# Two halves instead of one product: normalisation by head, inverse planes in another order, the last gate in two

## The chip, the core and the metric

The kernel runs on one core of one Trainium2 chip. The metric is the device time of a run in microseconds (us). Shorter is better.

## The reference

Local attention with a few global keys, followed by a gated long convolution. Four batches, 8 heads of 64, 768 positions, model width 512. What is computed, cut to its core:

```python
keep  = (pos_k < 8) | ((0 <= rel) & (rel < 96))        # rel = pos_q - pos_k
s     = q @ k.T / 8 - slope[h] * dist                   # dist: |rel|, or 96 for a far global key
a     = softmax(where(keep, s, -1e9))
x     = (a @ v) as [batch, 768, 512]
x1, x2, x3 = split(x @ w_proj)                          # three times 512 columns
conv  = irfft(rfft(x2, axis=1) * rfft(filter, axis=0)) # length 768
out   = (x1 * conv * x3) @ w_out
```

## The kernel before

**How the work is cut.** The program is a list of some thousand pieces ("atoms"), each a handful of instructions for one engine with a cost, the pieces it needs and a due number. A planner (`Plan.order`) walks through them: for each engine it takes the piece that can start first by its own reckoning, and among those within 30 of each other the one with the smallest number in the table `DUE`. A second table, `HOME`, pins some pieces that both ScalarE (ACT) and VectorE (DVE) could do to one of them. The result is one fixed order of instructions on each engine; on the chip every engine works through its own order and waits on semaphores. PSUM is one tile, `bank`, whose eight banks the planner hands out: single banks, and pairs of banks.

**The stages of a batch b.** Names in brackets are the planner's kinds, with the lines of the profile.

- Head of the program: GpSimd (POOL) writes two index rows and issues the loads. DVE makes distances in `far` (L324 to L344: the tile `neg`, then casts into `dist`, L331 and L332, a small strip, L333, and the rows of the global keys). TensorE (PE), ACT and DVE make the sines of the Fourier matrices (`wh`, L411, is a step of it on DVE; PE multiplies it in at L415). The filter, `fl`, is loaded by POOL at L499, folded by DVE (L516 to L526), multiplied by PE (L544) and copied to `h`. After the sines ACT makes the masks from `dist` (L359, L363).
- Queries and keys are transposed by PE (L697) and copied out as `QT`, `KT` (L225 on ACT, L227 on DVE: the helper `copy` records all plain copies on these lines, those with a factor on L225 and L229).
- For each of the four pairs of heads: scores (L857; for batch 0 the distances are added by PE at L845), exponentials by ACT (L874), masks by DVE (L885, batches 1 to 3), and the values (L899, L903) into a pair of banks, one bank for each head of the pair, with the sum of each row in a 65th column. Normalising is one piece on DVE: the reciprocal of 14 sums (L914) and one product over 128x896 (L915). PE transposes the result (L946), and ACT or DVE copies it to `xT`.
- After pairs 1 and 3 DVE folds the columns of two pairs (L965 to L970, tile `xr`). PE makes x1 and x3 from `xT` (L1056, "gates"), x2 from `xr` (L991), and the forward transform (L1009); copies `x`, `ab` and `X` leave the banks on ACT or DVE. DVE multiplies the spectrum (L1028 to L1040).
- The inverse: PE writes an even and an odd half for each 128 columns (L1118), each of three planes of 128; one copy takes both halves to `eo`; DVE completes the planes and joins the halves to `y` (L1152 to L1160: a sum of planes into `es`, a correction, and four sums or differences of halves) and multiplies by the gates (L1167). In the last batch this goes column block by column block.
- PE multiplies by `w_out` (L1182); the copy `ot` and a store by SyncE (SP, L1199) end the batch.

Of the kernel before, what the change touches and what calls it, by code (L numbers as in the profile page):

```python
# [30 lines left out]
class Plan:  # L31
# [9 lines left out]
    OPEN, SWAP, STICK = 8, 95.0, 1292.892  # L41
    LONE = 24718.4
# [138 lines left out]
class Fused:  # L181
# [134 lines left out]
    def far(self, part):  # L316
# [13 lines left out]
        if part == 1:  # L330
            v.tensor_copy(dist[:, 0:3], neg[:, None, :].to_broadcast([P, 3, 216]))  # L331
            v.tensor_copy(dist[:, 3, 0:168], neg[:, 0:168])  # L332
            v.tensor_scalar(dist[:, 3, 168:216], neg[:, 72:120], self.pc, None, op0=Alu.max)  # L333
        if part == 2:
            gl = mp.tile([NG, 2, KL], F32, tag="rc2", bufs=1, name="gl")
# [102 lines left out]
    def setup(self):  # L438
# [11 lines left out]
        for p, n in enumerate((1400, 1110, 2080)):  # L450
            A["far"] = [add("DVE", n, lambda p=p: self.far(p), [A["d0"]] + A["far"], due=-9, kind=f"far.{p}")]
# [275 lines left out]
    def due_hy(self, b, off):  # L727
# [3 lines left out]
    DUE = [2.91, 1.28, 8.39, 7.23, 4.07, 5.61, 7.59, 8.65, 5.7, 13.31, 5.58, 11.66, 13.01, 11.97,  # L731
# [529 lines left out]
```

## Time and profile before

| | |
|---|---|
| median of three runs | 173.18 us (173.03 to 173.38) |
| the profiled execution: its own time | 173.39 us |
| its span, first to last instruction | 171.6 us |
| granted TensorE clock | 1.000 |
| busy in the span | PE 93%, DVE 91%, ACT 81%, POOL 45% |

The profile gives each engine's busy time, the rows of a timeline (start and duration in us, engine, line, operation, output<-input), groups of equal instructions with their mean duration, and the chain of work that ended last. On ACT and DVE the next instruction of the same engine starts a little before the recorded end of the one ahead of it, so what an instruction costs its engine is read from the distance of two starts. A matmul's recorded duration holds its way through the array, and four matmuls can be under way at once.

### The profile page before, as it was taken

What the parts mean: (1) busy time and instruction counts of PE and PEld (TensorE: products, weight loads), DVE (VectorE), ACT (ScalarE), POOL (GpSimd) and SP (SyncE); (2) the same over time, 40 slices, a digit from 0 to 9 for tenths busy, and PEclk for the clock granted to TensorE, in tenths of its full rate; (3) what the DMA queues carried; (4) which work ended last, traced back from release to release, by engine and by line L of the source; (5) the groups of instructions that cost most, each with busy time, mean ns of one, the idle gap of its engine ahead of it and who ended that gap; (6) DMA issues with size and microseconds to landing.
All of it is one profiled execution on the core that took longest, in us unless ns stands there. A gap on an engine that the chain in (4) does not pass through costs nothing.

```text
span 171.6 us, 4147 instructions
## 1 busy us (share of the span) xinstructions
PE 159.0 (93%) x1595; PEld 94.1 (55%) x1595; DVE 156.5 (91%) x365; ACT 138.8 (81%) x244; POOL 77.9 (45%) x101
## 2 busy tenths in 40 slices
PE   5398979889999999999999999999999999999990
PEld 2046437675445777644566775454657754457630
DVE  7899989899999999999999999999999999999830
ACT  4479989899886849889997778988998988868751
POOL 8992885533999958632497768210000000000000
PEclk9999999999999999999999999999999999999999
DMA  3999999999999999999999999999921100062036
GB/s 47 152 149 186 125 178 182 206 205 159 123 116 118 130 136 146 106 160 126 129 150 215 165 184 164 108 101 150 271 97 65 63 0 0 35 253 85 0 132 234
DMA packets 81731, 22.97 MB, mean 134 GB/s; under 512 B 71536, under 2 KB 78640, under 8 KB 81712
## 3 DMA queue, kind: packets, MB, share of 16 engines
q0 software_dynamic: 64208, 12.81, 119.8%
q1 hardware_dynamic: 17504, 9.90, 31.0%
q8 instruction: 12, 0.20, 0.5%
q14 instruction: 7, 0.06, 0.1%
HBM read 25.59 MB, written 6.29 MB: 186 GB/s over the span
## 4 chain that ended last, share of the span: by engine, by line
PE 70%; DVE 23%; ACT 1%; issue 1%; POOL 1%; DVEq 0%; POOLq 0%; ACTq 0%
PE bank L1056 21%; PE bank L991 12%; PE bank L1182 10%; PE bank L1118 5%; PE bank L1009 5%; DVE xn L915 4%; PE bank L857 3%; PE bank L899 3%; DVE E L885 3%; PE bank L946 3%; PE bank L903 2%; PE bank L697 2%; DVE KT L227 2%; DVE QT L227 2%; PE bank L845 2%; PE bank L544 2%
## 5 line engine op out<-in xcount | busy, mean ns | idle before, releaser
L1056 PE MATMUL bank<-xT,w 128*128 128x384 f16 x256 | 47.6, 326 | 0.1
L874 ACT ACTIVATE E<-bank 128x864 f16<-128x864 f32 x48 | 41.1, 906 | 1.3 <-PE bank L857 1.3
L617 POOL DMA_DIRECT2D vb<-in_v_dram x32 | 27.2, 851 | 21.2 <-DMA vb<-in_v_dram 12.2
L1056 PEld LDWEIGHTS <-w 128*128 128x128 f16 x256 | 24.2, 98 | 16.6 <-issue 0.9
L225 ACT ACTIVATE x<-bank 128x384 f16<-128x384 f32 x52 | 25.9, 507 | 6.2 <-PE bank L1056 4.6
L991 PE MATMUL bank<-w,xr 128*128 128x512 f16 x96 | 23.1, 380 | 0.0
L1182 PE MATMUL bank<-wo,y 128*128 128x512 f16 x96 | 23.0, 379 | 0.0
L885 DVE TENSOR_TENSOR E<-E,mask 128x864 f16<-128x864 f16 x36 | 20.9, 599 | 0.4 <-ACT E L874 0.3
L915 DVE TENSOR_TENSOR xn<-bank,rc 128x896 f16<-128x896 f32 x16 | 17.5, 1092 | 0.6
L225 ACT ACTIVATE ot<-bank 128x512 f32<-128x512 f32 x22 | 13.2, 611 | 5.4 <-PE bank L1182 4.2
L225 ACT CAST ab<-bank 128x512 f16<-128x512 f32 x24 | 14.0, 594 | 3.6 <-PE bank L991 3.5
L663 POOL DMA_DIRECT2D q<-in_q_dram x16 | 13.6, 853 | 5.0 <-DMA wo<-in_moe_w_out_dram 1.8
L899 PEld LDWEIGHTS <-E 128*128 128x128 f16 x224 | 14.0, 98 | 2.0
L857 PE MATMUL bank<-QT,KT 64*128 64x216 f16 (+2 forms) x224 | 14.5, 242 | 0.7 <-ACT E L874 0.7
L663 POOL DMA_DIRECT2D k<-in_k_dram x16 | 13.8, 864 | 2.5 <-DMA k<-in_k_dram 2.2
L899 PE MATMUL bank<-vb,E 128*128 128x65 f16 x224 | 14.8, 193 | 0.0
L225 ACT CAST X<-bank 128x512 f16<-128x512 f32 x23 | 13.0, 603 | 2.1 <-PE bank L1009 2.0
L991 PEld LDWEIGHTS <-xr 128*128 128x128 f16 x96 | 8.9, 98 | 10.3 <-issue 0.9
L1182 PEld LDWEIGHTS <-y 128*128 128x128 f16 x96 | 9.0, 98 | 9.7 <-DVE y L1167 0.6
L903 PE MATMUL bank<-vb,E 128*128 128x65 f16 x192 | 14.3, 193 | 0.0
L225 ACT CAST eo<-bank 128x768 f16<-128x768 f32 x16 | 12.6, 812 | 1.7 <-PE bank L1118 1.6
L857 PEld LDWEIGHTS <-KT 64*128 64x128 f16 x224 | 7.9, 94 | 10.1 <-issue 6.8
(135 smaller groups left out, 298.0 us busy)
## 6 DMA issues: line engine op xcount, KB each, us to landing
out_dram<-ot SPq DMA_DIRECT2D x24, 256.0 KB, 2.3
vb<-in_v_dram POOLq DMA_DIRECT2D x32, 90.0 KB, 10.3
w<-in_moe_w_proj_dram POOLq DMA_DIRECT2D x3, 512.0 KB, 12.7
q<-in_q_dram POOLq DMA_DIRECT2D x16, 96.0 KB, 8.3
k<-in_k_dram POOLq DMA_DIRECT2D x16, 90.0 KB, 7.6
k<-in_k_dram POOLq DMA_DIRECT2D x4, 192.0 KB, 4.5
q<-in_q_dram POOLq DMA_DIRECT2D x4, 192.0 KB, 5.8
fl<-in_moe_filter_fft_dram POOLq DMA_DIRECT2D x1, 768.0 KB, 9.8
```

What stands on the lines that cost most here:

```text
L225: nc.scalar.copy(dst, src) if scale is None else nc.scalar.mul(dst, src, scale)
L617: g.dma_start(x[NG:P, 0:6, h, 0:D], self.v[b, h, 0:6 * KL].rearrange("(t p) d -> p t d", p=KL))
L663: g.dma_start(tile()[NG * j:P, i, 0:6, D * hh:D * hh + D], x.rearrange("(t p) d -> p t d", t=6))
L857: nc.tensor.matmul(sp[:, hh, off:off + w], KT[64 * hh:64 * hh + 64, o:o + P], QT[64 * hh:64 * hh + 64, KL * m:KL * m + w], start=(off == 0 ...
L874: nc.scalar.activation(eo, self.t["s", n, gi][:, :, 0:432].rearrange("p h (m w) -> p h m w", m=2), Act.Exp, scale=self.scale)
L885: nc.vector.tensor_mul(eo, eo, mk)
L899: nc.tensor.matmul(oc, ef[:, c:c + P], vt[:, t, 2 * i + hh, :], start=(t == 0), stop=(t == 0), skip_group_check=True)
L903: nc.tensor.matmul(oc, ef[:, c:c + P], vt[:, t - 1, 2 * i + hh, :], start=False, stop=True, skip_group_check=True)
L915: nc.vector.tensor_mul(xn.rearrange("p t h d -> p h t d"), o[:, :, :, 0:D], rc.to_broadcast([P, 2, 7, D]))
L991: nc.tensor.matmul(pt, T["xr", b][:, 2 * c + t // 3, t % 3], self.w[:, c, DM:2 * DM], start=(c == 0), stop=(c == 3))
L1056: nc.tensor.matmul(pt[:, 0:h], self.w[:, c, o + P * j:o + P * j + P], T["xT", b][:, c, h * s:h * s + h], start=(c == 0), stop=(c == 3))
L1182: nc.tensor.matmul(T["o", b, t], T["y", b][:, c, P * t:P * t + P], self.wo[:, c, :], start=(c == 0), stop=(c == 3))
```

## The change

Five edits, and two new tables. The constants `STICK` and `LONE` of the planner and both tables, `DUE` and `HOME`, are replaced as a whole, so the order on every engine differs nearly everywhere, though each piece's needs are the same but for the edits.

1. Normalising is three pieces: the reciprocal (still one, on DVE), and one product for each head of the pair, on DVE or on ACT. On ACT a product is seven instructions of 128x64 with the reciprocal as a scale read by each partition.
2. The two casts of the distances may go to ACT (`self.copy`), and the strip is a piece of its own.
3. The inverse's matmuls write their double plane to planes 0 and 2 and the single one to plane 1, so that joining the halves is three instructions in place of four.
4. In the last batch the last column block's copy to `eo` is two pieces, and its joining and gate are two parts, "a" for the planes 0 and 2 and "b" for plane 1.
5. The six output tiles of the last batch come in the order 1, 4, 0, 3, 2, 5.

```diff
-    OPEN, SWAP, STICK = 8, 95.0, 1292.892
-    LONE = 24718.4
+    OPEN, SWAP, STICK = 8, 95.0, 1434.540
+    LONE = 34987.8
...
-            v.tensor_copy(dist[:, 0:3], neg[:, None, :].to_broadcast([P, 3, 216]))
-            v.tensor_copy(dist[:, 3, 0:168], neg[:, 0:168])
+            self.copy(dist[:, 0:3], neg[:, None, :].to_broadcast([P, 3, 216]))
+            self.copy(dist[:, 3, 0:168], neg[:, 0:168])
+        if part == 3:
             v.tensor_scalar(dist[:, 3, 168:216], neg[:, 72:120], self.pc, None, op0=Alu.max)
...
-    DUE = [2.91, 1.28, 8.39, 7.23, 4.07, 5.61, 7.59, 8.65, 5.7, 13.31, 5.58, 11.66, 13.01, 11.97,
+    DUE = [0.69, -0.13, 5.71, 13.54, 2.85, 4.08, 8.43, 6.13, 11.65, 12.87, 3.67, 6.19, 7.33,
...
-            nc.vector.reciprocal(rc, o[:, :, :, D:D + 1])
-            nc.vector.tensor_mul(xn.rearrange("p t h d -> p h t d"), o[:, :, :, 0:D],
-                                 rc.to_broadcast([P, 2, 7, D]))
+            nc.vector.reciprocal(rc, o[:, :, :, D:D + 1])
...
+                if self.cur.eng == "ACT":
+                    for t in range(7):
+                        nc.scalar.activation(xn[:, t], o[:, t, 0:D], Act.Copy, scale=rc[:, t])
+                else:
+                    nc.vector.tensor_mul(xn, o[:, :, 0:D], rc.to_broadcast([P, 7, D]))
...
-                            nc.tensor.matmul(pt[:, P * lo:P * lo + P * n], xt(s), m, start=(s > 1 and s % 2 == 0),
+                            o3 = pt[:, 0:3 * P].rearrange("p (t m) -> p t m", t=3)
+                            nc.tensor.matmul(o3[:, 0:3:2] if n == 2 else o3[:, lo], xt(s), m, start=(s > 1 and s % 2 == 0),
...
-                    v.tensor_sub(yv[:, :, 1], eo[:, :, 0, 1], eo[:, :, 1, 1])
-                    v.tensor_add(yv[:, :, 4], eo[:, :, 0, 1], eo[:, :, 1, 1])
-                    v.tensor_add(yv[:, :, 0:3:2], eo[:, :, 0, 0:3:2], eo[:, :, 1, 0:3:2])
-                    v.tensor_sub(yv[:, :, 3:6:2], eo[:, :, 0, 0:3:2], eo[:, :, 1, 0:3:2])
+                        if part == "a":
+                            v.tensor_add(yv[:, :, 0:5:4], e[:, :, 0:3:2], o[:, :, 0:3:2])
+                            v.tensor_sub(yv[:, :, 3], e[:, :, 0], o[:, :, 0])
+                            v.tensor_sub(yv[:, :, 1], e[:, :, 2], o[:, :, 2])
+                        elif part == "b":
+                            v.tensor_add(yv[:, :, 2], e[:, :, 1], o[:, :, 1])
+                            v.tensor_sub(yv[:, :, 5], e[:, :, 1], o[:, :, 1])
+                        else:
+                            v.tensor_add(yv[:, :, 0:6:2], e, o)
+                            v.tensor_sub(yv[:, :, 3:6:2], e[:, :, 0:2], o[:, :, 0:2])
+                            v.tensor_sub(yv[:, :, 1], e[:, :, 2], o[:, :, 2])
...
-        for t in range(6):
+        for k, t in enumerate((1, 4, 0, 3, 2, 5) if fine and b in self.THRICE else range(6)):
```

What the order becomes at three places. First the head of the program, on DVE, from the distances to the last step of the sines (`wh`); `idm` are scaled identities, `gl` the rows of the global keys. Before:

```order
L328 TENSOR_TENSOR neg<-neg,d_96 128x216
L349 MEMSET E_70 128x2x6x16
L350 MEMSET E_70 128x2x80
L411 TENSOR_SCALAR wh<-th 128x512
L411 TENSOR_SCALAR wh<-th 128x256
L331 CAST dist<-neg 128x648
L332 CAST dist<-neg 128x168
L333 TENSOR_SCALAR dist<-neg,pc 128x48
L411 TENSOR_SCALAR wh<-th 128x512
L336 TENSOR_SCALAR gl<-d_96 8x120
```

And now:

```order
L328 TENSOR_TENSOR neg<-neg,d_96 128x216
L412 TENSOR_SCALAR wh<-th 128x256
L350 MEMSET E_72 128x2x6x16
L351 MEMSET E_72 128x2x80
L355 TENSOR_SCALAR idm<-ident 128x128 x4
L334 TENSOR_SCALAR dist<-neg,pc 128x48
L355 TENSOR_SCALAR idm<-ident 128x128 x2
L412 TENSOR_SCALAR wh<-th 128x512 x2
L355 TENSOR_SCALAR idm<-ident 128x128 x2
L337 TENSOR_SCALAR gl<-d_96 8x120
```

The two casts have left DVE; they stand on ACT between its first and second step of the sines. Second, the same stretch on POOL, which issues the loads one after the other (`q`, `k`, `vb` are the first batch's queries, keys and values, `fl` the filter). Before:

```order
L304 IOTA row 1x384
L588 DMA k_89<-in_k_dram 128x2x384
L300 IOTA d_96 128x216
L588 DMA k_89<-in_k_dram 128x2x384 x2
L604 DMA vb_85<-in_v_dram 8x8x64
L446 MEMSET k_90 8x512
L588 DMA q_87<-in_q_dram 128x2x384 x2
L499 DMA fl<-in_moe_filter_fft_dram 128x6x512
```

And now:

```order
L589 DMA q_87<-in_q_dram 128x2x384
L304 ISA
L304 IOTA row 1x384
L300 IOTA d_96 128x216
L589 DMA k_89<-in_k_dram 128x2x384
L589 DMA q_87<-in_q_dram 128x2x384
L589 DMA k_89<-in_k_dram 128x2x384 x2
L447 MEMSET k_89 8x512
L605 DMA vb_85<-in_v_dram 8x8x64
L612 DMA vb_85<-in_v_dram 120x8x64
L500 DMA fl<-in_moe_filter_fft_dram 128x6x512
```

A load of queries now stands ahead of the first index row, and one more load of values (`120x8x64`, 120 KB on the page) stands ahead of the filter. Third, the last two normalisations of the last batch, on DVE (`E` the exponentials under their mask, `g` the gates). Before:

```order
L1082 TENSOR_TENSOR g<-x 128x768
L885 TENSOR_TENSOR E_72<-E_72,mask 128x2x2x216 x2
L914 RECIPROCAL rc<-bank 128x14
L915 TENSOR_TENSOR xn<-bank,rc 128x2x7x64
L914 RECIPROCAL rc<-bank 128x14
L915 TENSOR_TENSOR xn<-bank,rc 128x2x7x64
L1082 TENSOR_TENSOR g<-x 128x768
```

And now, first DVE, then ACT from the first of that batch's halves on it:

```order
L889 TENSOR_TENSOR E_72<-E_72,mask 128x2x2x216 x3
L918 RECIPROCAL rc<-bank 128x14
L930 TENSOR_TENSOR xn<-bank,rc 128x7x64 x2
L918 RECIPROCAL rc<-bank 128x14
L1097 TENSOR_TENSOR g<-x 128x768
L930 TENSOR_TENSOR xn<-bank,rc 128x7x64
L229 TENSOR_SCALAR x<-bank 128x384
L227 COPY xT<-bank 128x768
```

```order
L928 ACTIVATE xn<-bank,rc 128x64 x7
L225 ACTIVATE x<-bank 128x384
L878 ACTIVATE E_70<-bank 128x2x2x216 x2
L225 ACTIVATE x<-bank 128x384 x2
L225 COPY xT<-bank 128x768
L878 ACTIVATE E_70<-bank 128x2x2x216
L928 ACTIVATE xn<-bank,rc 128x64 x7
L225 ACTIVATE x<-bank 128x384 x2
L878 ACTIVATE E_72<-bank 128x2x2x216 x3
L225 ACTIVATE x<-bank 128x384
```

One head of a pair stays on DVE and the other has gone to ACT, among the exponentials; a copy `x` and a copy `xT` have come to DVE. Over the whole program 10 of the 32 halves are on ACT (70 instructions) and 22 on DVE. In turn these copies out of the banks change engine: on DVE `ot` goes from 2 to 6, `X` from 1 to 3, `ab` from 0 to 2, `xT` from 5 to 8, `x` from 4 to 5, and the copies to `h` from 6 to 3; ACT has as many fewer or more.

More of the change, by code (lines that the diff above doesn't have):

```diff
@@ L1161, in hyena @@
-                three = b in self.THRICE
-                hv = add("DVE", (1320 if three else 1660) if one else (1970 if three else 2580), halves, need + A.get(("yfree", b - 1), []) + ys[-1:],
-                         due(20 + 4.5 * jp), kind=f"H{nm}")
-                A.setdefault(("eofree", 2 * b + jp), []).append(hv)
-                def gate(js=js):
-                    nc.vector.tensor_mul(T["y", b][:, js], T["y", b][:, js], T["g", b][:, js])
-                ys.append(add("DVE", 450 if one else 870, gate,
-                              [hv] + [gates[j, s] for j in range(js.start, js.stop) for s in range(2)],
-                              due(21 + 4.5 * jp), kind=f"Y{nm}"))
+                three = b in self.THRICE
@@ L1183, in fn @@
                                          start=(c == 0), stop=(c == 3))
-                need = [x, A["wo"]] + (ys[0:cs[-1] + 1] if fine else ys)
-                x = add("PE", 216 * len(cs), fn, need, due(27 + 0.9 * t), take=None if first else "mm",
+                last = cs[-1] + (cs[-1] == 3 and t % 3 == 2 and len(ys) == 5)
+                need = [x, A["wo"]] + (ys[0:last + 1] if fine else ys)
+                x = add("PE", 216 * len(cs), fn, need, due(27 + 0.9 * k), take=None if first else "mm",
                         kind=f"O{b}.{t}")
```

127 lines of the change are left out of this document (79 added, 48 removed), and 169 rows, old and new, of the table DUE.

## The prediction

> **What bounds the kernel now.** First the page's chain of work that ended last, by engine:
>
> ```profile
> PE 70%; DVE 23%; ACT 1%; issue 1%; POOL 1%; DVEq 0%; POOLq 0%; ACTq 0%
> ```
>
> Two engines share the bound, so an average says little. The table by stretches shows where each of them sets the pace; its columns are the length, then the busy time (and instructions) of PE, its weight loads, DVE, ACT and POOL.
>
> ```profile
> 17.60:40.70 23.10, 20.72 (x358) 13.40 (x357) 21.34 (x40) 21.23 (x38) 14.02 (x18) 1.00 1.89 181
> 40.70:44.00 3.30, 3.30 (x28) 1.80 (x28) 3.27 (x10) 2.80 (x5) 1.74 (x3) 1.00 3.63 120
> 44.00:118.00 74.00, 73.89 (x698) 43.54 (x694) 72.59 (x152) 62.00 (x108) 48.34 (x58) 1.00 2.23 141
> 118.00:134.00 16.00, 15.91 (x216) 10.27 (x213) 15.44 (x31) 14.63 (x25) 0.00 (x0) 1.00 0.79 152
> 134.00:168.00 34.00, 33.36 (x203) 18.71 (x203) 28.94 (x75) 26.27 (x48) 0.00 (x0) 1.00 0.19 72
> ```
>
> From 17.6 to 134 DVE idles 1.76 + 0.03 + 1.41 + 0.56 = 3.8 us of 116, and ACT 1.87 + 0.50 + 12.0 + 1.37 = 15.7 us. A PE that is busy there is not a PE at its peak, since a matmul is recorded longer than it holds the array. After 134 the picture turns: DVE idles 5 us, and the timeline has the last 24 products with `w_out` in one piece, then one copy and one store:
>
> ```profile
> 162.02 5.34 PE L1182 MATMUL bank<-wo,y 128*128 128x512 f16 x24
> 163.33 0.56 DVE L1167 TENSOR_TENSOR y<-y,g 128x768 f16<-128x768 f16 x1
> 167.45 0.60 ACT L225 ACTIVATE ot<-bank 128x512 f32<-128x512 f32 x1 [0.32 <-PE bank L1182]
> ```
>
> 24 products in 5.34 us, of which the last one's way through the array is a part, is 0.22 us each: nothing waits there. So I read: **to 134 us DVE's list sets the pace, with ACT behind it; after that PE's own work does**, about 34 us, then 4 us of copy and store, and none of that shrinks. The sum therefore goes over DVE's list up to the last normalisation.
>
> **The change part by part.** *Normalising.* In the last batch's timeline the next start shows what each instruction holds DVE for:
>
> ```profile
> 126.38 1.09 DVE L915 TENSOR_TENSOR xn<-bank,rc 128x896 f16<-128x896 f32 x1
> 127.40 0.61 DVE L885 TENSOR_TENSOR E<-E,mask 128x864 f16<-128x864 f16 x1
> 127.92 0.55 DVE L229 TENSOR_SCALAR x<-bank 128x384 f16<-128x384 f32 x1
> 128.39 0.41 DVE L1036 TENSOR_TENSOR X<-p,p 128x512 f16<-128x512 f16 x1
> ...
> L915 DVE TENSOR_TENSOR xn<-bank,rc 128x896 f16<-128x896 f32 x16 | 17.5, 1092 | 0.6
> ```
>
> The product takes 127.40 - 126.38 = 1.02 us for 896 elements, a copy of 384 from a bank 0.47. On the line through both, 448 elements take 0.54 (0.51 if it were plain half, 0.60 with one more start-up). So 16 x 1.02 = 16.3 becomes 22 x 0.54 = 11.9: **-4.4 us** (-5.1 to -3.1). The 16 reciprocals stay.
>
> *Copies that come to DVE.* A 512-wide one, and `xT`:
>
> ```profile
> 114.92 0.68 DVE L227 CAST X<-bank 128x512 f16<-128x512 f32 x1
> 115.52 0.68 DVE L1028 TENSOR_TENSOR p<-X,h 128x1024 f16<-128x1024 f16 x1
> ...
> 40.19 0.55 DVE L227 COPY xT<-bank 128x768 f16<-128x768 f16 x1
> 40.66 1.08 DVE L227 COPY KT<-bank 128x720 f16<-128x720 f16 x2
> ```
>
> 0.60 and 0.47 us. Up to the last normalisation DVE gets 4 `ot`, 2 `X` and 2 `ab` more, 8 x 0.60 = 4.8, two `xT` 0.94 (the third comes after it), one `x` 0.47, and three copies to `h` fewer, -1.8: **+4.4 us**. What normalising frees, other work takes.
>
> *Distances.* The casts leave DVE, where the sines waited behind them:
>
> ```profile
> 6.53 0.82 DVE L331 CAST dist<-neg 128x648 f16<-128x648 f32 x1
> ...
> 8.15 0.46 DVE L333 TENSOR_SCALAR dist<-neg,pc 128x48 f16<-128x48 f32 x1
> 8.30 0.57 DVE L411 TENSOR_SCALAR wh<-th 128x512 f16<-128x512 f32 x1
> ```
>
> Both casts lie between the first two rows, 8.15 - 6.53: **-1.6 us**. ACT takes them on; from its masks,
>
> ```profile
> L359 ACT ACTIVATE mask<-dist 128x432 f16<-128x432 f16 x8 | 4.2, 555 | 0.0
> L363 ACT ACTIVATE mask<-dist 128x216 f16<-128x216 f16 x8 | 2.8, 381 | 0.0
> ```
>
> 0.8 ns an element, about 0.9 us for both, while ACT is waiting for the sines. If DVE were no faster for it, ACT's second step of the sines would still come up to 0.9 late; the removed 1.6 covers that.
>
> *Planes of the inverse.* Two of the four joining instructions were 128x256, and two 128x512, for a pair of column blocks:
>
> ```profile
> L1157 DVE TENSOR_TENSOR y<-eo 128x256 f16<-128x256 f16 x6 | 1.7, 284 | 0.0
> L1160 DVE TENSOR_TENSOR y<-eo 128x512 f16<-128x512 f16 x6 | 2.5, 417 | 0.0
> L965 DVE TENSOR_TENSOR xe<-xT 128x768 f16<-128x768 f16 x8 | 4.4, 551 | 0.2
> ```
>
> Less the 0.08 by which neighbours overlap, 2 x 0.20 + 2 x 0.33 = 1.07 becomes 0.47 + 0.33 + 0.20 = 1.00. Four such groups lie ahead of the last normalisation: **-0.3 us**. That PE now leaves out a plane between two written ones I cost at nothing. In the chain of work, whose rows have start and length,
>
> ```profile
> 57.32 0.39 PE bank L946 x7
> 64.41 0.55 PE bank L1118 x6
> ```
>
> seven matmuls of 128 columns hold the array for 0.056 us each, and the inverse's six (four of 256, two of 128) for 0.55 together, so a double plane takes 0.11: even as two outputs of 128 it would cost no more.
>
> *Last gate and copy in two, tiles in another order.* DVE's last gate ends at 163.9, 1.9 us after the products began, and PE never stopped for it. So: nothing. The cover is the 18 products of `w_out` that need earlier column blocks; if it were gone, at most the length of joining and gate of plane 1, under 1 us. In parts, the gate costs one more start-up on an idle DVE.
>
> The sum over DVE's list is -4.4 + 4.4 - 1.6 - 0.3 = -1.9 us. **But not all of it counts.** On DVE the filter's fold is a fixed point, and the filter comes by DMA:
>
> ```profile
> 6.43 0.84 POOL L499 DMA_DIRECT2D fl<-in_moe_filter_fft_dram  x1
> 11.74 0.91 POOL L611 DMA_DIRECT2D vb<-in_v_dram  x1
> 16.54 0.84 POOL L617 DMA_DIRECT2D vb<-in_v_dram  x1 [3.06 <-DMA fl<-in_moe_filter_fft_dram]
> 17.59 0.94 DVE L516 TENSOR_TENSOR f<-fl 128x1536 f16<-128x1536 f16 x1
> ```
>
> The filter lands by 16.5 and the fold begins at 17.6, since DVE was not there before. Now POOL issues one more load of values (0.91 us, the second row) ahead of it, so it lands by about 17.45, and the fold, though DVE is free earlier, can come only 0.15 us sooner. Of the -1.9, the casts' -1.6 lie ahead of it; against that DVE does by its order one more `KT` there (1.08, in the row above), one more transposed matrix `inv` (17.07 to 17.59) and one `QT` less (half of the 1.82 below):
>
> ```profile
> 14.24 1.82 DVE L227 COPY QT<-bank 128x768 f16<-128x768 f16 x2 [0.30 <-PE bank L697]
> 17.07 0.48 DVE L431 COPY inv<-bank 128x640 f16<-128x640 f16 x1
> ```
>
> +0.7 together. So -0.9 lies ahead of the fold and is lost in a wait, and **-1.0 counts behind it, with 0.15: -1.2 us.** The profiled execution's 173.39 becomes 172.2; it stands 0.2 above the median, so the median of 173.18 becomes **172.0 us**.
>
> **What ACT pays.** The trace has no ACT instruction of 64 elements with a factor read from memory. The nearest are small copies:
>
> ```profile
> 120.17 0.26 ACT L225 COPY KT<-KT 128x56 f16<-128x56 f16 x1
> 120.30 0.63 ACT L225 ACTIVATE ot<-bank 128x512 f32<-128x512 f32 x1
> L225 ACT COPY KT<-KT 128x56 f16<-128x56 f16 x7 | 1.7, 249 | 0.0
> ```
>
> 56 elements hold ACT for 0.13 us if the next may overlap, and 0.25 if nothing does. I take 0.14 (the row nearest in size and way of use), 1.0 us for a half, bounds 0.9 to 1.75. Ten halves are 10 us (9 to 17.5); a 512-wide copy on ACT is the 0.63 of the second row less that overlap, 0.48, `x` at 0.8 ns an element 0.38 and `xT` 0.68, so what leaves ACT up to the last normalisation (8 x 0.48, 0.38 and 2 x 0.68, less 0.9 of casts and 3 x 0.48 for `h`) is 3.2. Net +6.5 (to +14) against ACT's 15.7 idle. It fits at my price; at the upper bound ACT is as full as DVE. What a half waits for is the reciprocal on DVE; behind it in ACT's queue stand a copy `x` and the next exponentials, so PE's scores and DVE's masks wait with it.
>
> The Trainium skill, "ScalarE: Activation LUTs", section "What ACT_TABLE_LOAD costs", gives an ACTIVATE with immediate factors 186 ns + 0.833 ns an element, about 93 ns overlap with its neighbour, and about 93 ns more for each operand read by partition. The first agrees with the masks' rows above (546 and 366 by it, 555 and 381 measured); of the last no run here shows anything yet. By it a piece is 239 ns, an estimate from that page, ten halves 16.7 us, and ACT stands near my upper bound, for which the slower rival below gives the time.
>
> **The rivals.**
>
> *More.* DVE's idle behind the fold, 1.76 us up to 40.7, is waiting for PE and ACT, and both come out of the sines earlier now. If it goes as well, 1.2 + 1.8 = 3.0, so 170.2. Against more than that speaks the weights' landing:
>
> ```profile
> 25.06 0.76 POOL L497 DMA_DIRECT2D w<-in_moe_w_proj_dram  x1
> ...
> DMA to landing us min/median/max: 11.6/12.7/13.8
> L1056 PE MATMUL bank<-xT,w x256: 322/326/337, 40.7 to 161.9; 128*128 128x384 f16 x128
> ```
>
> The gates began at 40.7; their first weights land at 25.06 + 12.7 = 37.8, with as many loads ahead of them as before. So 2.9 us is all that the head can give.
>
> *None.* If PE, not DVE, carries 44 to 134 (it is busy 89.8 of 90 us), the head's 1.2 us is won, but the 4.4 us of copies that come to DVE in the middle stand in other places than the products that left, and banks come free later there by as much: 173.2.
>
> *Slower.* ACT's pieces do not overlap. In the last batch's attention ACT idled 1.37 us (118 to 134). By ACT's order, five `ab`, an `X` and two `ot` (8 x 0.48), two `x` (0.76) and a small copy, 4.7 us, have gone from between that batch's first exponential and its last normalisation, and three halves have come. At 0.22 us a piece that is even; at 0.25 it is 0.6 too much (21 x 0.25 - 4.7), and the last half ends 1.75 - 1.02 = 0.7 later than the old product, with the last transposes and 34 us of PE behind it. With DVE's gain lost to it: 173.2 + 1.3 = 174.5. For it speaks that ACT's copies wait on banks rather than on time; against it that the small copy did overlap.
>
> **How the numbers follow.** Forecast 0.43, at 172.0 (171.3 to 173.3 on its own, by the bounds on DVE's half); more 0.23, at 170.2; none 0.10, at 173.2; slower 0.24, at 174.5. A measurement of this kernel tells about 0.2% (0.35 us) from no change. Faster is the second and nearly all of the first, 0.65; within 0.2% the third and the rest of the first, 0.11; slower 0.24. Leaving out a tenth on each side the range is 169.7 to 174.6.
>
> **What would show it.** L331 and L332 gone from DVE and the sines done 1 us sooner; the fold at about 17.4, behind a wait for `fl`; the first gate near 39.5; the last transposes of the last batch near 132.8, and from there the same 38 us to the end. ACT's `xn` rows starting 0.14 us apart confirm the price, 0.25 the slower rival. I am wrong if the fold starts much before 17.4, or if PE shows gaps behind ACT's halves.

## The result, and the profile after

The changed kernel takes **174.49 us** (median of 14 runs, 173.63 to 176.83) against 173.17 (14 runs, 173.00 to 173.45) of the kernel before: ratio **1.007, 95% interval 1.0048 to 1.0092**. It is slower by 0.7%, inside the range of the prediction and on the other side of its forecast. Where a run was disturbed on the chip it is left out of the ratios.

The page of the profiled execution (173.83 us, span 172.1), its busy times and its chain of work by engine:

```profile
PE 159.6 (93%) x1595; PEld 94.7 (55%) x1595; DVE 155.5 (90%) x371; ACT 147.7 (86%) x308; POOL 78.1 (45%) x101
...
PE 57%; DVE 15%; ACT 14%; DMA 6%; POOL 4%; issue 2%; POOLq 0%; DVEq 0%; ACTq 0%
```

ACT had 1% of the chain before and has 14% now, and a DMA stands in it with 6%. To see where the time went, cut the span at two instructions of PE: the first gate, and the last 24 products with `w_out`. In the timeline of the changed kernel:

```profile
39.58 1.47 PE L1071 MATMUL bank<-xT,w 128*128 128x384 f16 x8
162.35 5.60 PE L1220 MATMUL bank<-wo,y 128*128 128x512 f16 x24
```

Before, they began at 40.70 and 162.02. So the head is 1.12 us shorter, the middle 122.77 in place of 121.32 (**+1.45**), and the end 9.75 in place of 9.58 (+0.17): together the 0.5 us between the spans. The forecast had the first gain and nothing of the two losses. The time of this execution, 173.83 us, is 0.66 below the median of the 14 runs; a later head, as in the second profile below, is one way to the rest. The same table of stretches as before (length, then PE, weight loads, DVE, ACT, POOL):

```profile
17.60:40.70 23.10, 20.72 (x363) 14.28 (x362) 20.30 (x38) 22.47 (x47) 13.78 (x17) 1.00 1.84 177
40.70:44.00 3.30, 3.30 (x28) 1.87 (x26) 3.17 (x9) 3.25 (x7) 1.70 (x2) 1.00 2.21 145
44.00:118.00 74.00, 73.59 (x688) 43.06 (x686) 72.63 (x155) 65.85 (x142) 49.22 (x59) 1.00 2.03 143
118.00:134.00 16.00, 15.58 (x209) 10.23 (x208) 15.45 (x35) 15.35 (x40) 0.00 (x0) 1.00 0.83 141
```

DVE is as full as before, and ACT went from 14.63 to 15.35 of the 16 us of the last attention. The halves themselves, groups on ACT and on DVE, then one of them in ACT's timeline:

```profile
L928 ACT ACTIVATE xn<-bank,rc 128x64 f16<-128x64 f32 x70 | 15.3, 338 | 2.4 <-DVE rc L918 2.4
```

```profile
L930 DVE TENSOR_TENSOR xn<-bank,rc 128x448 f16<-128x448 f32 x22 | 13.1, 618 | 0.3
```

```profile
30.93 1.54 ACT L928 ACTIVATE xn<-bank,rc 128x64 f16<-128x64 f32 x7 [0.23 <-DVE rc L918]
```

Seven pieces of 0.338 us take 1.54, so a step is (1.54 - 0.34) / 6 = 0.20; the single starts are 0.196 us apart. A half on ACT costs 7 x 0.196 = **1.37 us**, not the 1.0 that the prediction took. On DVE a half is as forecast, 0.618 less the overlap of 0.08.

At the fold, DVE and then POOL, which issued the filter at 7.75:

```profile
17.55 0.96 DVE L517 TENSOR_TENSOR f<-fl 128x1536 f16<-128x1536 f16 x1 [0.15 <-DMA fl<-in_moe_filter_fft_dram]
```

```profile
7.75 0.86 POOL L500 DMA_DIRECT2D fl<-in_moe_filter_fft_dram  x1
...
17.82 1.80 POOL L618 DMA_DIRECT2D vb<-in_v_dram  x2 [3.30 <-DMA fl<-in_moe_filter_fft_dram]
```

The fold waits for the filter, as forecast, but begins at 17.55 and not at 17.4. In the kernel before the filter was there 1.05 us ahead of the fold (16.54 and 17.59); now the fold begins when the filter lands.

### The profile page after: what moved, and what is told of

Read it like the earlier page. It is cut to its first block, busy times and chain, and to the rows that moved or that the text cites. A ratio compares the mean times of both kernels' runs of the same rounds, so it can differ in the third digit from the quotient of the medians.

```text
span 172.1 us, 4240 instructions
## 1 busy us (share of the span) xinstructions
PE 159.6 (93%) x1595; PEld 94.7 (55%) x1595; DVE 155.5 (90%) x371; ACT 147.7 (86%) x308; POOL 78.1 (45%) x101
## 4 chain that ended last, share of the span: by engine, by line
PE 57%; DVE 15%; ACT 14%; DMA 6%; POOL 4%; issue 2%; POOLq 0%; DVEq 0%; ACTq 0%
PE bank L1071 18%; PE bank L1006 11%; PE bank L1220 6%; DMA fl<-in_moe_filter_fft_dram 6%; ACT E L878 5%; PE bank L1134 4%; ACT xn L928 4%; PE bank L861 3%; PE bank L961 3%; PE bank L1024 3%; PE bank L903 3%; DVE E L889 2%; PE bank L907 2%; ACT KT L225 2%; PE bank L545 1%
## 5 line engine op out<-in xcount | busy, mean ns | idle before, releaser
L225 ACT ACTIVATE x<-bank 128x384 f16<-128x384 f32 x51 | 24.8, 516 | 4.1 <-PE bank L1071 2.6
L928 ACT ACTIVATE xn<-bank,rc 128x64 f16<-128x64 f32 x70 | 15.3, 338 | 2.4 <-DVE rc L918 2.4
L225 ACT CAST ab<-bank 128x512 f16<-128x512 f32 x22 | 12.9, 588 | 4.9 <-PE bank L1006 4.3
L861 PE MATMUL bank<-QT,KT 64*128 64x216 f16 (+2 forms) x224 | 15.0, 242 | 1.7 <-DVE QT L227 1.0
L903 PE MATMUL bank<-vb,E 128*128 128x65 f16 x224 | 14.5, 193 | 0.0
L861 PEld LDWEIGHTS <-KT 64*128 64x128 f16 x224 | 8.6, 94 | 10.8 <-issue 7.9
L907 PE MATMUL bank<-vb,E 128*128 128x65 f16 x192 | 14.1, 193 | 0.0
L225 ACT CAST eo<-bank 128x768 f16<-128x768 f32 (+1 forms) x17 | 12.8, 789 | 1.0 <-PE bank L1134 0.7
L225 ACT ACTIVATE ot<-bank 128x512 f32<-128x512 f32 x18 | 10.6, 605 | 3.5 <-PE bank L1220 3.4
L930 DVE TENSOR_TENSOR xn<-bank,rc 128x448 f16<-128x448 f32 x22 | 13.1, 618 | 0.3
```

Source lines behind the costliest of these rows:

```text
L225: nc.scalar.copy(dst, src) if scale is None else nc.scalar.mul(dst, src, scale)
L861: nc.tensor.matmul(sp[:, hh, off:off + w], KT[64 * hh:64 * hh + 64, o:o + P], QT[64 * hh:64 * hh + 64, KL * m:KL * m + w], start=(off == 0 ...
L903: nc.tensor.matmul(oc, ef[:, c:c + P], vt[:, t, 2 * i + hh, :], start=(t == 0), stop=(t == 0), skip_group_check=True)
L907: nc.tensor.matmul(oc, ef[:, c:c + P], vt[:, t - 1, 2 * i + hh, :], start=False, stop=True, skip_group_check=True)
L928: nc.scalar.activation(xn[:, t], o[:, t, 0:D], Act.Copy, scale=rc[:, t])
```

## The experiments

**Theory 1: ACT's halves** cost more than they free. **Rival 1: the filter** (and with it the head) comes late. **Rival 2: the tail** loses at its end. Times of all runs stand beside runs of the kernel before on the same chip. "Head" is the start of the first gate, "middle" from there to the last 24 products, "end" the rest of the span, of the profiled execution.

| kernel | ratio to before (95% interval) | head | middle | end |
|---|---|---|---|---|
| before | 1 | 40.70 | 121.32 | 9.58 |
| changed | 1.007 (1.0048 to 1.0092) | 39.58 | 122.77 | 9.75 |
| changed, again | 1.0089 (1.006 to 1.0117) | 40.80 | 122.87 | 9.73 |
| half as one copy (0.43 us) | 0.9935 (0.9903 to 0.9967) | 39.26 | 121.30 | 9.84 |
| half with a constant factor (0.72) | 0.9962 (0.993 to 0.9994) | 39.07 | 121.28 | 9.75 |
| half at 1.0 us | 0.9974 (0.9945 to 1.0004) | 40.66 | 121.50 | 9.74 |
| three halves on DVE | 1.0058 (1.0033 to 1.0083) | 39.98 | 122.78 | 9.74 |
| all halves on DVE | 1.0246 (1.0208 to 1.0283) | 40.21 | 125.90 | 9.69 |
| trade undone | 1.0527 (1.0495 to 1.0559) | 41.60 | 128.22 | 9.68 |
| filter first | 1.0058 (1.003 to 1.0087) | 39.82 | 122.76 | 9.72 |
| filter first, joining turned | 1.0042 (1.0025 to 1.0058) | 39.82 | 122.45 | 9.73 |
| one output copy to DVE | 1.0078 (1.0049 to 1.0106) | 41.01 | 122.75 | 9.84 |
| last gate in one | 1.0096 (1.0083 to 1.0109) | 39.72 | 122.73 | 10.35 |
| before, half masks | 0.996 (0.9942 to 0.9979) | 40.32 | 120.78 | 9.60 |
| before, casts on ACT | 0.9965 (0.9946 to 0.9984) | 39.73 | - | - |
| before, planes | 1.0019 (1.001 to 1.0029) | 40.28 | 121.47 | 9.65 |
| before, casts and planes | 0.9991 (0.9976 to 1.0005) | 39.52 | 121.68 | 9.60 |
| the same, joining turned | 0.998 (0.997 to 0.9989) | 39.79 | - | - |

The two dashes stand where the profiled execution took the longest of its kernel's times. One of them shows what a single execution can hold: with the casts on ACT its middle is 122.21, 0.89 more than before though the order there is the same, and 0.7 of that comes between 88 and 92 us. In the changed kernel the middle of one order repeats within 0.14 us (122.73 to 122.87 in the five rows that leave it as it is), so a loss of 1.45 is read safely there; a difference of 0.15 between two single executions is not.

**The changed kernel again.** No edit.

> The changed kernel once more, beside the runs below. All theories: the time of before plus 0.7% (174.5 against 173.2 us), and if the wide spread of its runs (173.6 to 176.8) belongs to the kernel, again over 2 us between its fastest and slowest run, where before has less than 0.5.

174.88 us (174.33 to 175.65): slower again. The spread was not as expected: these six runs lie within 1.3 us, and those of the kernel before beside them within 1.6 (172.97 to 174.57). The middle is the same, the head 1.2 later than in the first profile. The fold in this execution, and the next transposes of queries on PE:

```profile
18.35 0.96 DVE L517 TENSOR_TENSOR f<-fl 128x1536 f16<-128x1536 f16 x1 [1.09 <-DMA fl<-in_moe_filter_fft_dram]
```

```profile
22.03 0.53 PE L698 MATMUL bank<-ident,q 128*64 128x128 f16 x12 [0.70 <-DMA q<-in_q_dram]
```

The load issued at 7.75 in both landed 0.8 us later here, and a load of queries behind it 0.7 late. The gain of the head is there in some executions and gone in others.

**Half as one copy.**

```diff
-                    for t in range(7):
-                        nc.scalar.activation(xn[:, t], o[:, t, 0:D], Act.Copy, scale=rc[:, t])
+                    nc.scalar.copy(xn, o[:, :, 0:D])
```

> The changed kernel, but each half that ACT normalises is one plain copy of 448 elements in place of seven instructions of 64 with a factor (the division by the sums is left out in those ten halves); the order is the same. Theory 1, ACT's halves: the profile has a half at 1.37 us, a plain copy of 448 would be about 0.43 by the 512-wide copies, so ACT has 9.4 us less to do, and at the three places where PE stood behind such halves (31 to 33, 91.8 and 121.3 us) some 0.5 us each comes back: 173.2 to 172.5 us, and these gaps gone from PE. Rival 1, the filter: the fold waits for its DMA whatever ACT does: within 0.3 of the changed kernel, with its spread. Rival 2, the tail: the loss of 0.5 us behind the last products stays, and nothing else was lost: within 0.3 of the changed kernel.

172.53 us, the lower end of what theory 1 gave. The order is the same, the middle loses 1.47, and from the fold to the first gate it is 21.52 us (17.74 to 39.26) in place of 22.03:

```profile
L927 ACT CAST xn<-bank 128x448 f16<-128x448 f32 x10 | 5.3, 531 | 3.0 <-DVE rc L918 2.8
```

```profile
39.26 1.47 PE L1070 MATMUL bank<-xT,w 128*128 128x384 f16 x8
160.56 5.59 PE L1219 MATMUL bank<-wo,y 128*128 128x512 f16 x24
```

Both rivals fall as the main cause: neither the filter nor the tail was touched.

**Half at the price of the prediction.**

```diff
-                    for t in range(7):
+                    for t in range(4):
                         nc.scalar.activation(xn[:, t], o[:, t, 0:D], Act.Copy, scale=rc[:, t])
+                    nc.scalar.copy(xn[:, 4:7], o[:, 4:7, 0:D])
```

> The changed kernel, but each half on ACT is four pieces of 64 with the factor and one plain copy of 192 (in those ten halves the division by the sums is left out for the last three of seven). By the changed kernel's rows a piece is 0.196 us and a plain copy of 192 about 0.2, so the half costs 0.99 us: the 1.0 that the prediction took for it. If only the price was wrong in the prediction, the time is the forecast 172.0, or at most that of before (173.2). If a half on ACT is waited for whatever its price, the time lies between the one-piece run (0.43 us a half, 172.5) and the changed kernel (1.37 us, 174.9) in proportion: 173.9.

Ratio 0.9974 (0.9945 to 1.0004), which is 172.7 us; the median of all twelve runs is 173.56. The middle is 121.50:

```profile
40.66 1.47 PE L1072 MATMUL bank<-xT,w 128*128 128x384 f16 x8
162.16 5.59 PE L1221 MATMUL bank<-wo,y 128*128 128x512 f16 x24
```

So not in proportion, as I had expected if the price alone were not it: 0.57 us between 0.43 and 1.0 cost the middle 0.20, the 0.37 between 1.0 and 1.37 cost 1.27. With the half at its forecast price the change is by its ratio no slower than before. (The profiled execution, whose fold began late, at 18.14, and whose head is 40.66, took 173.65.)

**Half with a constant factor.**

```diff
-                        nc.scalar.activation(xn[:, t], o[:, t, 0:D], Act.Copy, scale=rc[:, t])
+                        nc.scalar.activation(xn[:, t], o[:, t, 0:D], Act.Copy, scale=0.125)
```

> The changed kernel, but the seven pieces of a half on ACT have a constant as factor in place of one read by partition (the division by the sums is left out in those ten halves). If the operand by partition is what makes a piece 0.196 us: about 0.10 us from start to start, a half 0.73, and the time between the one-piece run and the run at 1.0 us a half, 172.6 to 173. If it is the way from the bank: 0.19 us as before, and the time of the changed kernel.

```profile
L928 ACT ACTIVATE xn<-bank 128x64 f16<-128x64 f32 x70 | 9.1, 250 | 2.7 <-DVE rc L918 2.5
...
30.92 0.92 ACT L928 ACTIVATE xn<-bank 128x64 f16<-128x64 f32 x7 [0.23 <-DVE rc L918]
```

```profile
39.07 1.47 PE L1071 MATMUL bank<-xT,w 128*128 128x384 f16 x8
160.35 5.59 PE L1220 MATMUL bank<-wo,y 128*128 128x512 f16 x24
```

A piece lasts 0.250 in place of 0.338, and the single starts are 0.103 apart in place of 0.196. The factor read by each partition is nearly half of what a piece holds ACT for. Middle 121.28, the floor that the one-piece run has too: below 1.0 us a half costs the middle about 0.2.

**All halves on DVE** and **the trade undone.** In the loop that emits the pieces:

```diff
         for _, self.cur in self.plan.order():
+            if self.cur.kind.startswith("N") and self.cur.kind[1].isdigit():
+                self.cur.eng = "DVE"
```

> The changed kernel, but all 32 halves are on DVE, each at its place in the order of pieces; ACT has ten halves less (13.7 us), DVE ten more (10 x 0.54 = 5.4 us). If DVE's list set the pace up to 134 us, as the prediction said: 3 to 5 us slower than the changed kernel, 177.5 to 180. If what was lost is PE's waits behind ACT's halves and DVE has the room: 172.5 to 174.

177.73 us, the middle 3.1 longer: in this order DVE had no room. For the trade, the 31 copies that had changed engine go back as well (22 to ACT; the expectation counts one too few):

> The changed kernel in its own order of pieces, with the trade of engines undone between the head and the last stage: all 32 halves on DVE, and the copies that had gone from one of ACT and DVE to the other back on their engine of before (21 come back to ACT, 9 to DVE). Against the changed kernel DVE has 10 x 0.54 more for halves and twelve copies at about 0.55 fewer, -1 us, and ACT 10 x 1.37 less and twelve at about 0.5 more, -8 us. If the trade is the loss: as the one-piece run or better, 172 to 173. If the changed order itself is the loss, whoever does the pieces: 174 to 175, or more, since the order was not made for this division.

182.0 us, far off all that I expected. By the busy times DVE had 0.6 us less to do and ACT 5.9 us less than in the changed kernel (154.9 and 141.8), and yet the middle grew by 5.5. The order of the pieces was made for another division, and I take it that pieces which come to an engine at a place not made for them hold it up; no run shows this by itself. The run says nothing on the trade, and it weakens the reading of the run ahead of it in the same way.

**Three halves on DVE.**

```diff
+            if self.cur.eng == "ACT" and self.cur.kind in ("N0.2", "N2.1", "N3.1"):
+                self.cur.eng = "DVE"
```

> The changed kernel, but three of the ten halves on ACT are done by DVE: that of the first batch (30.9 us), one of the two that follow each other at 89.6, and that at 120.5, behind each of which PE waited some 0.5 us. If PE's waits behind these halves are the loss: 1.0 to 1.5 us faster than the changed kernel, 173.2 to 173.8. If DVE has no room for 3 x 0.54 in a list made without them (as all ten on DVE cost 3 us): the time of the changed kernel or more, 174.5 to 175.5.

174.15 us, ratio 1.0058, not told apart from the changed kernel; the middle is the same to 0.01. PE's waits in the changed kernel had looked like the place of the loss:

```profile
PE bank L861 <- ACT xn L928: 0.7, 2, 0.4
PE bank L698 <- ACT KT L225: 0.5, 1, 0.5
```

The run does not test this as meant. The piece `N3.1` that it moved is the half that began at 126.19, not the one at 120.55, which stayed on ACT; and of the two at 89.49 the second, still on ACT, now began at 91.20, behind a later reciprocal. So PE waits at both places as before. The changed kernel, then this run:

```profile
92.51 0.35 PE L861 MATMUL bank<-QT,KT 64*128 64x216 f16 x5 [0.27 <-ACT xn L928]
122.14 0.34 PE L861 MATMUL bank<-QT,KT 64*128 64x216 f16 x3 [0.39 <-ACT xn L928]
```

```profile
92.90 0.36 PE L861 MATMUL bank<-QT,KT 64*128 64x216 f16 x6 [0.40 <-DVE xn L930]
122.57 0.34 PE L861 MATMUL bank<-QT,KT 64*128 64x216 f16 x3 [0.39 <-ACT xn L928]
```

The run at 1.0 us a half answers the question. It has the same 1595 matmuls in the same order, so each can be set against the same one of the changed kernel. Of the 1.27 us between the two middles, 0.5 comes at 92.5 and 0.4 at 122.1, the very two waits behind ACT's halves; another 0.2 comes at 60.5. In the rows of the run at 1.0 us PE does not wait at these two places:

```profile
92.86 0.56 PE L861 MATMUL bank<-QT,KT 64*128 64x216 f16 x10
121.77 0.90 PE L861 MATMUL bank<-QT,KT 64*128 64x216 f16 x8
```

With the constant factor the same two places give 0.3 and 0.6 of 1.49. In the last attention the stretch of the run with three halves on DVE reads

```profile
118.00:134.00 16.00, 15.61 (x206) 10.01 (x205) 15.76 (x36) 14.19 (x31) 0.00 (x0) 1.00 0.64 137
```

ACT is down to 14.19, and DVE up to 15.76 of 16: what leaves the one full engine fills the other.

**Half masks, in the kernel before.** This asks for the first step of the prediction, that DVE's list sets the pace to 134 us.

```diff
-                    nc.vector.tensor_mul(eo, eo, mk)
+                    nc.vector.tensor_mul(eo[:, :, 0:1], eo[:, :, 0:1], mk[:, :, 0:1])
```

> The kernel before, but each of the 36 products of exponentials and mask covers one half of its columns (the mask is left out on the other half): 432 elements in place of 864, about 0.27 in place of 0.52 us, 9 us less on DVE between 44 and 134 us with the order and the waits as they were. If DVE's list sets the pace there, as the prediction said: 4 us or more faster, below 169. If PE sets it and DVE only keeps up: less than 1 us, 172.3 to 173.3.

The products in the kernel before, then in this one:

```profile
L885 DVE TENSOR_TENSOR E<-E,mask 128x864 f16<-128x864 f16 x36 | 20.9, 599 | 0.4 <-ACT E L874 0.3
```

```profile
L885 DVE TENSOR_TENSOR E<-E,mask 128x432 f16<-128x432 f16 x36 | 13.2, 378 | 2.6 <-ACT E L874 2.3
```

```profile
40.32 1.47 PE L1056 MATMUL bank<-xT,w 128*128 128x384 f16 x8
161.10 5.34 PE L1182 MATMUL bank<-wo,y 128*128 128x512 f16 x24
```

36 x (0.599 - 0.378) = 8.0 us less on DVE shortened the middle by 0.54 and the time by 0.4%. DVE waits instead, for the exponentials (2.6 us of idle ahead of this group) and for other work of ACT and PE. So DVE's list alone does not set the pace: a gain on it is given back at the next wait. Whether PE or ACT sets it, the run does not show.

**Filter first.**

```diff
+        fl = next(a for a in out if a.kind == "ldf")
+        out.remove(fl)
+        out.insert(out.index(next(a for a in out if a.kind == "ldv0.g")), fl)
```

> The changed kernel, but POOL issues the filter's load ahead of the first batch's two loads of values, about 1.5 us earlier, as early as in the kernel before. Rival 1, the filter: the fold no longer waits in any run; the spread of the runs falls below 1 us and the median to that of the fastest runs or below it, 173.0 to 173.7. Theory 1, ACT's halves: in the profiled execution the fold waited only 0.15 us for the DMA, so the median falls by 0.2 at most and the spread stays. The values come later by this; if they are waited for, the first values product (PE, near 26 us) shows it.

174.08 us, and the fold begins without a wait, at 17.80. The median came down by 0.4 against the better of the two sets of runs of the changed kernel, less than rival 1 had (173.7 or below), more than theory 1 had (0.2), and within what the intervals allow as chance. The spread did not go: 173.68 to 176.49. What spreads the changed kernel's runs is not the filter alone. In its profiled executions the spread lies in the head, not in the middle: in the first profile, in the run with the last gate in one, in the repeat and in the run with an output copy on DVE, PE waited 0.2, 0.6, 1.4 and 1.6 us for loads of queries (`in_q_dram`), and the heads are 39.58, 39.72, 40.80 and 41.01. What the longest times, up to 176.8 us, are made of stays open, since none of them has a profile.

**One output copy to DVE.**

```diff
+            if self.cur.kind == "EO3.4":
+                self.cur.eng = "DVE"
```

> The changed kernel, but the last output copy but one (tile 2 or 5 in the new order, whichever the planner put ahead of the last) is on DVE in place of ACT, so that the two last copies run side by side and not one after the other on ACT. Rival 2, the tail: the last store starts 0.45 us sooner and the median falls by 0.4 to 0.5 us. If the time goes by something else than the last copy (the store's own latency, or the last products themselves), less than 0.2.

175.05 us, no gain, and the end is 9.84, no shorter. The last copy of this run waited for PE, not for the copy ahead of it:

```profile
169.44 0.60 ACT L225 ACTIVATE ot<-bank 128x512 f32<-128x512 f32 x1 [0.75 <-PE bank L1220]
```

**Last gate in one.** Joining and gate of the last column block stand whole where part a stood, and part b does nothing.

```diff
-                        if part != "a":
+                        if part != "b":
                             z = mp.tile([P, 4, P], F16, tag="es", bufs=1, name="es")[:, 0:2 * n]
...
-                        nc.vector.tensor_mul(y, y, g)
+                        if part != "b":
+                            nc.vector.tensor_mul(y, y, g)
```

> The changed kernel, but the last column block is joined and gated in one piece at the place of part a (the copy to the halves stays in two, and the output tiles in their new order). If the split is why PE's last products wait 0.25 us (they stood behind part b's gate): that gap gone and 0.2 to 0.3 us faster, unless the first products now wait instead for the later single gate. If the split helps: slower by the 0.6 us by which the single gate ends later than part a.

The end is 10.35, 0.6 longer than with the split. First the changed kernel, where PE's last weights wait for part b, then this run:

```profile
165.05 0.29 DVE L1205 TENSOR_TENSOR y<-y,g 128x256 f16<-128x256 f16 x1
...
165.40 2.06 PEld L1220 LDWEIGHTS <-y 128*128 128x128 f16 x11 [0.57 <-DVE y L1205]
```

```profile
165.10 2.92 PEld L1210 LDWEIGHTS <-y 128*128 128x128 f16 x15 [1.04 <-DVE y L1195]
```

The split helps where it stands. In the changed kernel PE's gap of 0.25 us (0.46 between two products' starts in place of 0.216) lies ahead of the fourteenth of the 24 products, the first that needs part b.

**Casts, planes, and the sequence of the joining, in the kernel before.** The casts:

```diff
-            v.tensor_copy(dist[:, 0:3], neg[:, None, :].to_broadcast([P, 3, 216]))
-            v.tensor_copy(dist[:, 3, 0:168], neg[:, 0:168])
+            self.nc.scalar.copy(dist[:, 0:3], neg[:, None, :].to_broadcast([P, 3, 216]))
+            self.nc.scalar.copy(dist[:, 3, 0:168], neg[:, 0:168])
```

> The kernel before, with the two casts of the distances on ACT and nothing else changed (1.6 us less on DVE ahead of the sines and the fold). The filter lands at 16.5 us there and the fold begins at 17.6: if the head's gain reaches the end, it is up to 1.05 us, 172.2 to 172.7. If it is given back in the middle as in the changed kernel, less than 0.3, 172.9 to 173.4. Slower, above 173.6, if ACT's masks or sines come late by the casts.

172.64 us, 0.9965 (0.9946 to 0.9984): an edit of the change that pays alone, and a version faster than both kernels. Then the planes alone (the change's edit 3 without the split), and both:

> The kernel before with only the planes of the inverse reordered (three joining instructions in place of four). By the prediction 0.07 us for each of six pairs of column blocks on DVE, at most -0.3 us at the end: 172.8 to 173.2; PE's product over the planes 0 and 2 lasts as long as over 0 and 1 (0.11 us). If the gap between the planes costs PE, each such product lasts longer and the time is above 173.4.

> The kernel before with the casts of the distances on ACT and the reordered planes of the inverse, and nothing else of the change. The casts alone gave 0.5 us. Planes as the prediction costed them: 0.3 us more, 172.3; if PE takes longer for a product over two planes with one between: slower than the casts alone, 172.8 or more.

The planes cost: 1.0019 (1.001 to 1.0029), in the profiled executions +0.15 in the middle and +0.07 at the end. With the casts 0.9991, so here too they seem to take back a part of what those give. The other reading, that PE pays for the gap between the planes, falls by the traces: a product over two planes lasts 273 ns on the mean before and 272 with the planes reordered, and its neighbour starts 0.109 us after it in both. The joining on DVE, first in the kernel before, then with the planes:

```profile
72.79 0.42 DVE L1156 TENSOR_TENSOR eo<-eo,es 128x512 f16<-128x512 f16 x1
73.13 0.29 DVE L1157 TENSOR_TENSOR y<-eo 128x256 f16<-128x256 f16 x1
...
74.32 0.96 DVE L1167 TENSOR_TENSOR y<-y,g 128x1536 f16<-128x1536 f16 x1
```

```profile
72.36 0.42 DVE L1158 TENSOR_TENSOR eo<-eo,es 128x512 f16<-128x512 f16 x1
72.82 0.56 DVE L1159 TENSOR_TENSOR y<-eo 128x768 f16<-128x768 f16 x1
...
73.95 0.96 DVE L1168 TENSOR_TENSOR y<-y,g 128x1536 f16<-128x1536 f16 x1
```

Before, the row behind the correction began 0.34 after it, ahead of its recorded end, since it reads another plane. Now the sum of all planes reads the plane that the correction writes, and begins 0.46 after it, 0.04 behind that end. One instruction less, and still 1.59 us from the correction to the gate in place of 1.53. Turned:

```diff
-                    v.tensor_add(yv[:, :, 0:6:2], e, o)
-                    v.tensor_sub(yv[:, :, 3:6:2], e[:, :, 0:2], o[:, :, 0:2])
                     v.tensor_sub(yv[:, :, 1], e[:, :, 2], o[:, :, 2])
+                    v.tensor_sub(yv[:, :, 3:6:2], e[:, :, 0:2], o[:, :, 0:2])
+                    v.tensor_add(yv[:, :, 0:6:2], e, o)
```

> The kernel before with the casts on ACT and the reordered planes, as in the run of these two, but the three joining instructions are written in the other sequence: the difference of plane 2 first, then the two differences, then the sums of all planes. In the run of planes alone the sum began 0.03 us after the end of the correction that writes plane 1, which it reads, where in the kernel before the next instruction read another plane and began 0.08 before that end: 0.117 us more for each of ten groups, 1.2 us of DVE. If this wait on the neighbour is why the planes cost 0.3 us in place of saving 0.3: the gap gone, and 172.2 to 172.6, as the casts alone or better. If the planes cost something else: 172.9 as with both edits.

```profile
72.06 0.42 DVE L1158 TENSOR_TENSOR eo<-eo,es 128x512 f16<-128x512 f16 x1
72.40 0.28 DVE L1159 TENSOR_TENSOR y<-eo 128x256 f16<-128x256 f16 x1
...
73.52 0.96 DVE L1168 TENSOR_TENSOR y<-y,g 128x1536 f16<-128x1536 f16 x1
```

The wait is gone and the way is 1.46 us, 0.07 less than before, as the prediction had it. The time, 172.73 us (0.998), is 0.1% under the run of casts and planes (0.9991), which the intervals do not tell apart. It lies above the 172.2 to 172.6 that was expected, though the intervals do not tell it from the casts alone (0.9965) either. That the wait is gone is shown; that the time follows it is not. In the changed kernel:

> The changed kernel with the filter's load ahead of the values' (as in the run of that alone, 174.1) and the joining in the turned sequence. If both are separate losses: 173.5 to 173.9. If ACT's halves set the pace whatever DVE saves: 174.1 as with the filter alone.

173.76 us, and the middle 122.45 in place of 122.76 with the filter alone: 0.3 us from the sequence of three lines, read from two single executions. The ratios (1.0042 and 1.0058) do not tell the two apart.

## Why the prediction was wrong, step by step

- **What a half costs on ACT: the step that failed.** "I take 0.14 (the row nearest in size and way of use), 1.0 us for a half." It is 0.196 and 1.37. That was inside the bounds given (0.13 to 0.25), but the forecast stood on the lower end. Ten halves at 1.0 leave the middle at 121.50, and at 1.37 at 122.77: **this term is 1.27 of the 1.45 us** that the middle lost, and at 1.0 us a half the run stands at 172.7 us by its ratio, inside the forecast's own range. Two waits of PE's scores behind ACT's halves carry 0.9 of the 1.27. These gaps are the sign of being wrong that the prediction named itself. The small copy of 56 elements from which the price was taken has no factor; with a constant factor a piece of 64 takes 0.103, so it is the factor read by each partition that was left out.
- **"It fits at my price"**, by 15.7 us of ACT's idle time: at 1.0 us a half it did fit (middle 121.50), but the measure was wrong. At 1.37 us ACT still shows 0.63 + 0.05 + 8.15 + 0.65 = 9.5 us of idle in the same stretches, and the loss was there: ACT idles 0.31 ahead of the half at 120.55, waiting for the reciprocal, and then PE waits 0.39 for that half. Idle time that is spent in waits is no room.
- **"To 134 us DVE's list sets the pace": wrong as a bound.** 8.0 us less on DVE gave 0.54 in the middle. In the other direction it is not free: 5.4 us more, in an order not made for it, cost 3.1.
- **Normalising against copies, -4.4 and +4.4: consistent, not shown by itself.** With the half at its price the middle is 121.50, that is 0.18 from before, and the planes alone gave 0.15, both about what a single execution varies by. That fits a draw on DVE, for which ACT paid; the run that was to undo the trade does not say.
- **Casts and the filter: right, but with no margin.** "The fold ... can come only 0.15 us sooner" (0.04 in the profile after), "the first gate near 39.5" (39.58), the sines a microsecond sooner (the last step of their matrix starts at 8.69 on ACT, before at 9.55): all there in the first profile. But "lands by about 17.45" was a fixed number for something that moves: the fold that waits for it began at 17.55 and at 18.35 in two executions, with a load of queries 0.70 late in the second. That the gain "behind the fold" is 1.0 came true in the one (22.03 us from the fold to the first gate, before 23.11) and not in the other (22.45). The head before moves too: in the runs with half masks and with the planes alone, which leave it as it is, it is 40.32 and 40.28, so against those the gain is 0.7. The casts alone, in an order with slack for the filter, give 0.35%.
- **Planes, -0.3: wrong sign.** The overlap of neighbours was taken for granted; the sum must wait for the line ahead of it. 0.33 us slower by the ratio. PE's gap between the planes, put at nothing, cost nothing (0.109 us a product in both), and turning three lines took DVE's wait away; how much of the 0.33 that wait is, stays open.
- **"Last gate and copy in two ... So: nothing": mis-sized**, by 0.17 of the end. The cover named was 18 products on PE; in the trace 13 ran before one needed part b, and PE stood 0.25 us there.
- **The slower rival** had the right engine and sign; that its figure (174.5) is the one measured is luck. It put the break-even at 0.22 us a piece and all of the loss in the last attention. At the measured 0.196 its own sum gives ACT a gain there (21 x 0.196 = 4.1 against 4.7), and the loss came at a few places from 60 to 135 us.

Open: by which waits the smaller part of the 1.27 us reaches PE, and what beyond the loads of the head spreads the changed kernel's times over 2 to 3 us.

## What to carry to other kernels

Before work is traded between two engines that are both nearly full, price it on both, with the exact form (operands and source) and not with the nearest copy; an engine's idle time counts as room only where you know what it waits for. When instructions are fused, ask whether the fused one reads what the line ahead of it has just written: an independent line between them can be worth more than the instruction saved. A piece that gives up its slack to a DMA takes over the DMA's spread.

## What the runs showed of the hardware

- A factor read by each partition adds 0.093 us to an ACT instruction of 64 elements from a bank (0.196 against 0.103 from start to start), nearly as much as such a piece takes without it. The Trainium skill, "ScalarE: Activation LUTs", section "What ACT_TABLE_LOAD costs", has about 93 ns for it, which these runs confirm. By that section's 186 ns and its overlap of 93 ns between neighbours a step would be an estimated 239 ns, which is too much. The Trainium skill, "Perfetto Trace Analysis", section "Optimizing Scalar/DVE Operations", has an overhead of about 51 ns for a ScalarE instruction on PSUM; with this in place of 186 - 93, an estimate from both pages is 51 + 53 + 93 = 197 ns, and 196 is what was measured.
- On DVE, in this kernel's joining, an instruction that reads what its neighbour wrote begins 0.034 us after the other's recorded end (0.104 in two of the ten joinings with the planes alone); one that doesn't, 0.08 ahead of it. The difference is 0.12 us.
- The same DMA, issued at 7.75 us, let DVE begin at 17.55 in one execution and at 18.35 in another.
